# Seeding a PSUM bank with the epsilon term of an RMS norm, and one warm-up product less

## The chip, the cores and the metric

One core of one Trainium2 chip runs the whole program. The metric is the device time of one execution in microseconds (us); lower is better. A profiled execution gives a trace with one record for each instruction.

## The reference

```python
kv  = einsum('bhsd,bhse->bhde', k, v)            # q, k, v: 8 x 8 x 576 x 64, fp32
out = einsum('bhsd,bhde->bhse', q, kv)
rms = sqrt(mean(out * out, axis=-1) + 1e-06)     # over the 64 elements of a head
x   = (out / rms * g_norm)                       # reshaped to 4608 tokens x 512
h   = x @ w_in                                   # 512 x 2048
y   = 0.5 * h * (1 + erf(h / sqrt(2))) @ w_out   # gelu, then 2048 x 512
```

It is a linear attention without softmax, an RMS norm over each head, and a feed-forward layer.

## The kernel before

The 4608 tokens are cut into nine chunks of 512. For a chunk, `Attn` makes the transposed attention output in four head pairs `p` (128 partitions are two heads of 64, 512 columns are tokens), norms it, and splits the normed values into a high and a low part, on which the feed-forward layer runs: `layer1` (or `layer1_pair`) into `ps_h` banks, `gelu`, and `layer2` into four `acc` banks. The weights come as raw 64-bit words and are converted on the chip during the first chunk (`top_w` on ScalarE, `bits_w` on VectorE, `high_w` on ScalarE, `low_w` on VectorE). While one chunk runs through the feed-forward layer, the attention of the next is done between the products. The instructions of each engine run in the order in which the program issues them; nothing reorders them.

The first chunk has nothing to hide behind, and its attention is written out by hand before the loop. This is the stretch that the change touches:

1. `keep_warm(10)` issues ten products of a tile of zeros into a bank that nobody reads (`dummy`). A product of fp32 operands is two passes of TensorE, each with its own weight load, so these are 20 passes. Meanwhile GpSimd fills small constants (`mask`, `heads`, `ident`, `fold`), and the loads of k, v and q are on their way.
2. For each head pair `p`, `sum_first(p)` sums k times v over the batch's rows (line 145) and masks the result into `kv_f` on VectorE (line 622); `project_first(p)` multiplies it with q (line 630) and squares the result on ScalarE (line 634). A one-column product (line 649) turns `g_norm` into a per-partition scalar, `half_g` (line 650).
3. The sums of the squares of pairs 0 and 1 come from VectorE's `reduce` and a product with `fold` (line 665), those of pairs 2 and 3 from products with `heads` in `sum_squares` (line 641). All of them lie in one PSUM bank, `sums`: 48 columns, each written by a product that starts and ends its own sum.
4. `rsqrt` (lines 240 to 268) takes the inverse roots on VectorE: `m` = sums / 64 + epsilon (line 247), a first guess from the bits of `m` (line 250), and two polynomial refinements (`stt` at line 256, products with `m` at lines 261 and 265). That is nine instructions, each of which needs the one before.
5. TensorE meanwhile issues `keep_warm(2)`, the sums of k times v of the second batch (line 145 again), and `keep_warm(2)` once more. Then line 687 spreads the roots of pairs 2 and 3 over the tokens with 16 products with `ident`, 32 passes. VectorE spreads those of pairs 0 and 1 (line 277) and applies all of them (lines 695 and 705), and `layer1` starts on the normed values (line 512 for the first two of its blocks, in plain fp32).

Of the kernel before, what the change touches and what calls it, by code (L numbers as in the profile page):

```python
# [8 lines left out]
F32 = mybir.dt.float32  # L9
F32R = mybir.dt.float32r  # L10
I32 = mybir.dt.int32
AF = mybir.ActivationFunctionType
ALU = mybir.AluOpType
# [3 lines left out]
P = 128  # L17
EPS = 1e-6
# [17 lines left out]
def linear_attn_rms_gelu_ffn(  # L36
# [16 lines left out]
    nc = tc.nc  # L53
# [6 lines left out]
    D = g_norm.shape[0]  # L60
    NF = w_in.shape[0]
# [4 lines left out]
    const = ctx.enter_context(tc.tile_pool(name="const", bufs=1))  # L66
# [12 lines left out]
    half_g = const.tile([P, 1], F32, name="half_g")  # L79
    heads = const.tile([P, 2], F32, name="heads")  # L80
# [4 lines left out]
    def late_tile(name):  # L85

        if name not in late:
            late[name] = const.tile([P, 2 * DM], I32, name=name).bitcast(F32)
        return late[name]
# [45 lines left out]
    def sum_kv(b, pairs, ps=None):  # L135

        first = 0 if ps is not None else pairs[0]
        if ps is None:
            ps = kv_ps[b, first] = ps_a.tile([P, 512], F32, name="ps_a")
        for p in pairs:  # L140
            n = p - first
            for j, (k, v) in enumerate(kv_in.pop((b, p))):

                for r in (slice(0, D), slice(D, 2 * D)):
                    nc.tensor.matmul(  # L145
                        out=ps[r, n * D:(n + 1) * D], lhsT=k[:, r], rhs=v[:, r],
                        start=(j == 0), stop=(j == NJ),
                    )
# [12 lines left out]
    class Attn:  # L161
# [76 lines left out]
            )  # L238
            return ps

        def rsqrt(self, ps):

            m, y, t = (
                work.tile([P, NP * NB], F32, name=a, bufs=2)[:, :ps.shape[1]]
                for a in ("m", "y", "t")
            )
            nc.vector.tensor_scalar(
                out=m, in0=ps, scalar1=1.0 / D, scalar2=EPS, op0=ALU.mult, op1=ALU.add
            )
            nc.vector.tensor_scalar(  # L250
                out=y.bitcast(I32), in0=m.bitcast(I32), scalar1=-0.5, scalar2=RSQRT_MAGIC,
                op0=ALU.mult, op1=ALU.add,
            )

            def stt(out, in0, c, op0, in1):
                nc.vector.scalar_tensor_tensor(
                    out=out, in0=in0, scalar=c, in1=in1, op0=op0, op1=ALU.mult
                )

            stt(t, y, RSQRT_S2, ALU.mult, y)  # L260
            nc.vector.tensor_tensor(out=t, in0=t, in1=m, op=ALU.mult)
            stt(t, t, RSQRT_D1, ALU.add, t)
            stt(y, t, RSQRT_D0, ALU.add, y)
            stt(t, y, -0.125, ALU.mult, y)
            nc.vector.tensor_tensor(out=t, in0=t, in1=m, op=ALU.mult)
            stt(y, t, 1.5, ALU.add, y)
            return y
# [201 lines left out]
    def top_w(n):  # L469


        zs[n] = work.tile([P, DM], I32, name="z", bufs=2)
        top = raw[n].rearrange("p (n two) -> p n two", two=2)[:, :, 1]
        if n < FULL:
            z = late_tile(f"w_out{NF - 1}")[:, n * DM:(n + 1) * DM]
        else:
            z = work.tile([P, DM], F32, name="w", bufs=2)
        nc.scalar.activation(
            out=zs[n].bitcast(F32), in_=top.bitcast(F32), func=AF.Prelu,
            scale=2.0 ** -112, alpha=2.0 ** 32,  # L480
        )
        ws[n] = z.bitcast(I32)
# [79 lines left out]
    first, second = attn[:2]  # L562
    nc.vector.memset(warm, 0.0)
    nc.scalar.activation(out=heads, in_=warm[:, :2], func=AF.Gelu)
    mask, g_row = late_tile(f"w_in{NF - 6}")[:, :P], late_tile(f"w_in{NF - 6}")[:1, P:2 * P]
    nc.gpsimd.memset(mask, 0.0)
    for r in (slice(0, D), slice(D, 2 * D)):
        nc.gpsimd.memset(mask[r, r], 1.0)
    load_kv(0, 0)
# [26 lines left out]
    def keep_warm(count):  # L596
        for _ in range(count):
            nc.tensor.matmul(out=dummy[:, :P], lhsT=warm, rhs=warm, start=True, stop=True)  # L598

    sums = ps_h.tile([P, CH], F32, name="ps_h")  # L600
# [2 lines left out]
    nc.gpsimd.memset(heads, 0.0)  # L603
    for h in range(2):
        nc.gpsimd.memset(heads[h * D:(h + 1) * D, h:h + 1], 1.0)
    make_identity(nc, ident)
    for d in range(0, 2 * D, BLK):
        h = d // D * D
        nc.gpsimd.tensor_tensor(
            out=fold[:, d:d + BLK], in0=ident[:, h:h + BLK], in1=ident[:, h + BLK:h + 2 * BLK],  # L610
# [7 lines left out]
    sq, NG = {}, CH // P  # L618

    def sum_first(p):  # L620
        sum_kv(0, (p,))
        nc.vector.tensor_tensor(
            out=kv_f[:, p].rearrange("p (a n) -> p a n", a=2),
            in0=kv_ps.pop((0, p))[:, :D].unsqueeze(1).broadcast_to((P, 2, D)),
            in1=mask.rearrange("p (a n) -> p a n", a=2), op=ALU.mult,
        )

    def project_first(p):
        first.ps[p] = ps_acc.tile([P, DM], F32, name=f"acc{p}")
        nc.tensor.matmul(  # L630
            out=first.ps[p], lhsT=kv_f[:, p], rhs=first.q.pop(p), start=True, stop=True
        )
        sq[p] = work.tile([P, CH], F32, name=SQ[p], bufs=2 if p == 3 else None)
        nc.scalar.activation(out=sq[p], in_=first.ps[p], func=AF.Square)

    n = 2 * NB


    def sum_squares(p):
        for k in range((p - 2) * NG, (p - 1) * NG):  # L640
            nc.tensor.matmul(  # L641
                out=sums[:, n + 2 * k:n + 2 * k + 2],
                lhsT=sq[p][:, k % NG * P:(k % NG + 1) * P], rhs=heads, start=True, stop=True,
            )

    first.part = work.tile([P, NP, NB], F32, name="part")
    sum_first(0)
    ps = ps_a.tile([P, 512], F32, name="ps_a")
    nc.tensor.matmul(out=ps[:, :1], lhsT=g_row, rhs=heads[:1, :1], start=True, stop=True)
    nc.vector.tensor_scalar(  # L650
        out=half_g, in0=ps[:, :1], scalar1=0.5, scalar2=None, op0=ALU.mult
    )
    project_first(0)
    sum_first(1)
# [5 lines left out]
    for p in (2, 3):  # L660
        project_first(p)
    top_w(0)
    bits_w(0)
    sum_squares(2)
    nc.tensor.matmul(  # L665
        out=sums[:, :n].rearrange("p (g b) -> p g b", g=2), lhsT=fold, rhs=first.part[:, :2, :],
        start=True, stop=True,
    )
    sum_squares(3)
    for p in (2, 3):  # L670
        nc.scalar.activation(
            out=first.o_tile(p), in_=first.ps.pop(p), func=AF.Copy, scale=half_g
        )
    top_w(1)
    first.inv = first.rsqrt(sums[:, :n + 4 * NG])

    keep_warm(2)
    kv_ps[1, 0] = ps_a.tile([P, 512], F32, name="ps_a")
    sum_kv(1, (0, 1), kv_ps[1, 0])
    keep_warm(2)  # L680
    bcs = {}
    for p in (2, 3):
        bcs[p] = ps_acc.tile([P, DM], F32, name=f"acc{p}")
        for t in range(NG):
            for h, r in enumerate((slice(0, D), slice(D, 2 * D))):
                k = n + 2 * ((p - 2) * NG + t) + h
                nc.tensor.matmul(  # L687
                    out=bcs[p][r, t * P:(t + 1) * P],
                    lhsT=first.inv[:, k:k + 1].broadcast_to((P, D)), rhs=ident,
                    start=True, stop=True,  # L690
                )
    for p in range(2):
        bc = work.tile([P, CH], F32, name=SQ[p])
        first.spread(p, bc)
        nc.vector.scalar_tensor_tensor(
            out=first.o_tile(p), in0=first.ps.pop(p), scalar=half_g, in1=bc, op0=ALU.mult,
            op1=ALU.mult,
        )
        first.high_x(p)
        if p == 0:  # L700
            first.low_x(0, nc.gpsimd)
            top_w(2)
# [10 lines left out]
    g, h, acc, sums = {}, {}, {}, {}  # L713
# [121 lines left out]
    for s in range(PLAIN * NF):  # L835
# [36 lines left out]
        else:  # L872
# [3 lines left out]
            n = 0 if not 1 <= i <= 11 else 2 if i in (1, 3, 5, 7, 11) else 1  # L876
# [116 lines left out]
```

## Time and profile before

| | us |
|---|---|
| three runs | 836.53, 839.05, 838.25 |
| median of the three | 838.25 |
| the profiled execution | 836.58 |
| its span, first instruction to last | 834.80 |
| outside of the span | 1.78 |

The three runs lie 2.5 us apart, which is 0.3%. The span is what the trace shows; the time outside it is before the first and after the last instruction. TensorE passes are pipelined, so the length that the trace gives for one pass is longer than the distance between the starts of two, and the distance is what a pass costs in a row of them.

### The profile page before, as it was taken

To read this page: it belongs to the slowest core of one execution; us is meant where nothing else is said; L and a number is where in the kernel's file an instruction comes from. 1 tells how busy PE (TensorE), PEld (TensorE's weight loads), DVE (VectorE), ACT (ScalarE), POOL (GpSimd) and SP (SyncE) were. 2 spreads that over 40 slices of the span, in tenths; PEclk is the share of its full clock that TensorE was granted. 3 is DMA by queue.
4 is the path that set the end of the run, shared out by engine and by line. 5 is a ranking of instruction groups with operands and counts; after the bars stand their busy time and mean duration, and the time that the engine had idled before them with its cause. 6 is when DMAs were issued, how large, how long until landed. Compare 5 with 4: busy or idle time off the path is not lost.

```text
span 834.8 us, 13786 instructions
## 1 busy us (share of the span) xinstructions
PE 829.1 (99%) x5380; PEld 734.7 (88%) x5380; DVE 495.3 (59%) x980; ACT 314.2 (38%) x580; POOL 65.2 (8%) x67
## 2 busy tenths in 40 slices
PE   8999999999999999999999999999999999999998
PEld 7688888888999999999999999999999989999997
DVE  3999838687546744674457545673467446744442
ACT  2788444434531334233423253233323332322221
POOL 1000021011010101010001010010101000100000
PEclk9999999999999999999999999999999999999999
DMA  9981337776684568456955587456455655556551
GB/s 350 406 328 51 114 123 258 255 247 239 242 313 131 175 237 302 165 177 202 325 172 174 203 275 263 148 181 231 172 170 174 214 202 177 177 177 227 177 177 50
DMA packets 61460, 174.96 MB, mean 210 GB/s; under 512 B 6484, under 2 KB 15188, under 8 KB 61396
## 3 DMA queue, kind: packets, MB, share of 16 engines
q1 hardware_dynamic: 61392, 174.09, 59.8%
q8 instruction: 42, 0.69, 0.3%
q14 instruction: 22, 0.18, 0.1%
q10 hardware_dynamic: 4, 0.00, 0.0%
HBM read 149.95 MB, written 24.12 MB: 209 GB/s over the span
## 4 chain that ended last, share of the span: by engine, by line
PE 98%; DMA 1%; ACT 0%; issue 0%
PE acc L546 47%; PE ps_h L427 34%; PE ps_h L520 10%; PE ps_a L205 3%; PE ps_a L145 2%; DMA w_out<-kv_main 1%; PE ps_h L512 1%; PE acc L687 0%; PE acc L630 0%; PE ps_h L641 0%; PE ps_a L235 0%; PE ps_h L598 0%; ACT z L557 0%; PE ps_h L665 0%
## 5 line engine op out<-in xcount | busy, mean ns | idle before, releaser
L546 PE MATMUL acc<-w_out,gh 128*128 128x512 f32 x704 | 218.4, 392 | 0.0
L427 PE MATMUL ps_h<-w_in,w_in 128*128 128x256 f32 x1392 | 176.2, 283 | 0.0
L427 PEld LDWEIGHTS ps_h<-w_in,w_in 128*128 128x128 f32 x1392 | 171.1, 192 | 0.0
L546 PE MATMUL acc<-w_out,w_in 128*128 128x512 f32 x672 | 159.7, 392 | 0.0
L546 PEld LDWEIGHTS acc<-w_out,gh 128*128 128x128 f32 x704 | 130.1, 188 | 25.5
L546 PEld LDWEIGHTS acc<-w_out,w_in 128*128 128x128 f32 x672 | 124.1, 188 | 24.7
L546 PE MATMUL acc<-w_out,gl 128*128 128x512 f32 x352 | 137.2, 390 | 0.0
L532 ACT ACTIVATE gh<-ps_h 128x512 fp32r<-128x512 f32 x88 | 52.5, 597 | 212.6 <-DVE ps_h L419 155.3
L427 PEld LDWEIGHTS ps_h<-x,w_in 128*128 128x128 f32 x960 | 122.6, 191 | 4.4
L427 PE MATMUL ps_h<-x,w_in 128*128 128x256 f32 x960 | 123.9, 283 | 0.0
L532 ACT ACTIVATE w_in<-ps_h 128x512 fp32r<-128x512 f32 x56 | 33.5, 598 | 184.8 <-DVE ps_h L419 184.8
L437 DVE COPY w_in<-ps_h 128x256 f32<-128x256 f32 x56 | 23.8, 425 | 133.2 <-PE ps_h L427 133.2
L419 DVE TENSOR_TENSOR ps_h<-ps_h,w_in 128x256 f32<-128x256 f32 x168 | 72.7, 433 | 48.0 <-PE ps_h L427 43.6
L419 DVE TENSOR_TENSOR w_in<-ps_h,w_in 128x256 f32<-128x256 f32 x168 | 71.4, 425 | 49.1 <-PE ps_h L427 47.2
L520 PE MATMUL ps_h<-x,w_in 128*128 128x512 f32 x360 | 86.8, 390 | 0.0
L538 DVE TENSOR_TENSOR gl<-ps_h,gh 128x512 fp32r<-128x512 f32 x88 | 60.5, 687 | 42.7 <-ACT ps_h L533 38.2
L533 ACT ACTIVATE ps_h<-ps_h 128x512 f32<-128x512 f32 x144 | 85.4, 593 | 0.0
L520 PEld LDWEIGHTS ps_h<-x,w_in 128*128 128x128 f32 x360 | 67.5, 188 | 13.9 <-POOL x L290 0.2
L546 PEld LDWEIGHTS acc<-w_out,gl 128*128 128x128 f32 x352 | 66.1, 188 | 14.1
L538 DVE TENSOR_TENSOR w_in<-ps_h,w_in 128x512 fp32r<-128x512 f32 x56 | 38.5, 687 | 17.0 <-ACT ps_h L533 17.0
L193 POOL TENSOR_TENSOR ql<-q,qh 128x512 fp32r<-128x512 f32 x16 | 21.3, 1328 | 211.0 <-ACT qh L192 116.0
L325 POOL TENSOR_TENSOR w_in<-o,w_in 128x512 fp32r<-128x512 f32 x13 | 16.8, 1311 | 212.3 <-ACT w_in L320 212.3
(135 smaller groups left out, 635.5 us busy)
## 6 DMA issues: line engine op xcount, KB each, us to landing
w_in<-products SPq DMA_DIRECT2D x196, 512.0 KB, 4.7
products<-w_in SPq DMA_DIRECT2D x40, 256.0 KB, 3.2
kv_main<-kv_main SPq DMA_DIRECT2D x18, 512.0 KB, 6.7
w_in<-w_in SPq DMA_DIRECT2D x16, 512.0 KB, 10.2
w_out<-w_out SPq DMA_DIRECT2D x16, 512.0 KB, 10.2
q<-qT SPq DMA_DIRECT2D x15, 512.0 KB, 6.3
out<-w SPq DMA_DIRECT2D x18, 256.0 KB, 2.1
out<-z SPq DMA_DIRECT2D x18, 256.0 KB, 2.2
```

Of the source, the lines that this page charges most:

```text
L145: nc.tensor.matmul(out=ps[r, n * D:(n + 1) * D], lhsT=k[:, r], rhs=v[:, r], start=(j == 0), stop=(j == NJ),)
L193: eng.tensor_tensor(out=ql, in0=q, in1=qh.bitcast(F32), op=ALU.subtract)
L205: nc.tensor.matmul(out=ps[:, a:e], lhsT=w, rhs=x[:, a:e], start=(m == 0), stop=(m == 2))
L325: eng.tensor_tensor(out=x[:, 1], in0=self.block(OPERANDS[n]), in1=x[:, 0].bitcast(F32), op=ALU.subtract,)
L419: add = lambda out, x, y: nc.vector.tensor_tensor(out=out, in0=x, in1=y, op=ALU.add)
L427: nc.tensor.matmul(out=out, lhsT=y, rhs=x[:, z, kb], start=first and kb + i == 0, stop=kb == 1 and i == 2, skip_group_check=True,)
L437: nc.vector.tensor_copy(out=p1, in_=a[:, left])
L520: nc.tensor.matmul(out=h, lhsT=parts["in", i][:, w][:, p * P:(p + 1) * P], rhs=at.x[p][:, x], start=(m + p == 0), stop=(m == 2 and p == NP ...
L532: nc.scalar.activation(out=gh, in_=h, func=AF.Gelu)
L533: nc.scalar.activation(out=h, in_=h, func=AF.Gelu)
L538: nc.vector.tensor_tensor(out=gl, in0=h, in1=gh.bitcast(F32), op=ALU.subtract)
L546: nc.tensor.matmul(out=ps, lhsT=x[:, ts], rhs=parts["out", i][:, w], start=(i == 0 and m == 0), stop=(i == NF - 1 and m == 2),)
```

## The change

A row of ones and a row of 64 times epsilon are filled by GpSimd. One product of the two, with one row of contraction, writes 64 times epsilon into all 48 columns of `sums` before the first sum; the sums of squares then accumulate on it. `rsqrt` takes its roots from that bank as it stands, which gives roots smaller by the factor 8 (the square root of 64), and a scalar `root_g` = 8 times `half_g` takes the place of `half_g` where the first chunk is scaled. The second `keep_warm(2)` becomes `keep_warm(1)`.

```diff
-        def rsqrt(self, ps):
+        def rsqrt(self, ps, ready=False):
...
-            nc.vector.tensor_scalar(
-                out=m, in0=ps, scalar1=1.0 / D, scalar2=EPS, op0=ALU.mult, op1=ALU.add
-            )
+            if ready:
+                m = ps
+            else:
+                nc.vector.tensor_scalar(
+                    out=m, in0=ps, scalar1=1.0 / D, scalar2=EPS, op0=ALU.mult, op1=ALU.add
+                )
...
+    ones, eps = (late_tile(f"w_in{NF - 6}")[:1, a * P:(a + 1) * P] for a in (2, 3))
...
+    nc.gpsimd.memset(ones, 1.0)
+    nc.gpsimd.memset(eps, D * EPS)
     make_identity(nc, ident)
...
-                lhsT=sq[p][:, k % NG * P:(k % NG + 1) * P], rhs=heads, start=True, stop=True,
+                lhsT=sq[p][:, k % NG * P:(k % NG + 1) * P], rhs=heads, start=False, stop=True,
+                skip_group_check=True,
...
+    nc.tensor.matmul(
+        out=sums[:, :n + 4 * NG], lhsT=ones, rhs=eps[:, :n + 4 * NG], start=True, stop=False,
+        skip_group_check=True,
+    )
     sum_first(0)
...
+    root_g = const.tile([P, 1], F32, name="root_g")
+    nc.vector.tensor_scalar(
+        out=root_g, in0=half_g, scalar1=D ** 0.5, scalar2=None, op0=ALU.mult
+    )
     project_first(0)
...
         out=sums[:, :n].rearrange("p (g b) -> p g b", g=2), lhsT=fold, rhs=first.part[:, :2, :],
-        start=True, stop=True,
+        start=False, stop=True, skip_group_check=True,
...
-            out=first.o_tile(p), in_=first.ps.pop(p), func=AF.Copy, scale=half_g
+            out=first.o_tile(p), in_=first.ps.pop(p), func=AF.Copy, scale=root_g
...
-    first.inv = first.rsqrt(sums[:, :n + 4 * NG])
+    first.inv = first.rsqrt(sums[:, :n + 4 * NG], True)
...
     sum_kv(1, (0, 1), kv_ps[1, 0])
-    keep_warm(2)
+    keep_warm(1)
...
-            out=first.o_tile(p), in0=first.ps.pop(p), scalar=half_g, in1=bc, op0=ALU.mult,
+            out=first.o_tile(p), in0=first.ps.pop(p), scalar=root_g, in1=bc, op0=ALU.mult,
```

## Rows read from the trace of the kernel before

**Rows 1.** The page of the profile: busy time and share of the span by engine, and the shares of the chain of work that ended last by engine.
```profile
PE 829.1 (99%) x5380; PEld 734.7 (88%) x5380; DVE 495.3 (59%) x980; ACT 314.2 (38%) x580; POOL 65.2 (8%) x67
PE 98%; DMA 1%; ACT 0%; issue 0%
```

**Rows 2.** All waits of TensorE between 12 us and the end of the span: who waited for whom, us in total, times, longest.
```profile
PE ps_a L145 <- DMA w_out<-kv_main: 0.2, 1, 0.2
```

**Rows 3.** The chain of work that ended last, in order of time, from 4 to 28 us: start, length, what.
```profile
4.34 7.31 DMA w_out<-kv_main
11.64 0.14 issue
11.78 0.80 PE ps_a L145 x20
...
18.42 0.64 PE ps_h L598 x4
19.06 1.96 PE acc L687 x32
21.02 7.15 PE ps_h L512 x16
```

**Rows 4.** VectorE in order of time, 15.7 to 20.4 us: start, length, line, operation, tiles; in brackets the idle time before and what ended it (none where there is no bracket).
```profile
16.18 0.69 DVE L491 SCALAR_TENSOR_TENSOR w_out<-w_in,w_out 128x512 int32<-128x512 int32 x1
16.78 0.20 DVE L247 TENSOR_SCALAR m<-ps_h 128x48 f32<-128x48 f32 x1
17.02 0.19 DVE L250 TENSOR_SCALAR y<-m 128x48 int32<-128x48 int32 x1
...
18.46 0.21 DVE L265 TENSOR_TENSOR t<-t,m 128x48 f32<-128x48 f32 x1
18.70 0.21 DVE L256 SCALAR_TENSOR_TENSOR y<-t,y 128x48 f32<-128x48 f32 x1
18.94 0.71 DVE L277 STREAM_TRANSPOSE sq<-y 128x512 f32<-128x512 f32 x1
```

**Rows 5.** TensorE's passes (PE) and weight loads (PEld) in order of time, 15.2 to 21 us, neighbours of one kind merged (xcount).
```profile
15.27 0.30 PEld L665 LDWEIGHTS ps_h<-part,fold 128*128 128x128 f32 x2
15.52 1.03 PE L641 MATMUL ps_h<-heads,gh 128*128 128x2 f32 x8
16.39 0.53 PEld L598 LDWEIGHTS ps_h<-warm 128*128 128x128 f32 x4
18.35 0.52 PEld L598 LDWEIGHTS ps_h<-warm 128*128 128x128 f32 x4
18.35 0.71 PE L598 MATMUL ps_h<-warm 128*128 128x128 f32 x4
19.02 1.75 PEld L687 LDWEIGHTS acc<-ident,y 128*64 128x64 f32 x32 [0.15 <-issue]
20.95 0.30 PEld L512 LDWEIGHTS ps_h<-o,w_out 128*128 128x128 f32 x2 [0.17 <-issue]
```

**Rows 6.** Two lines of `rsqrt` over the whole span: ns shortest/median/longest, first and last start, shapes and their counts. The bank `ps_a` or `ps_h` is PSUM, `m` is SBUF.
```profile
L247 DVE TENSOR_SCALAR m<-ps_a x8: 215/215/225, 91.2 to 697.2; 128x64 f32<-128x64 f32 x8
L247 DVE TENSOR_SCALAR m<-ps_h x1: 201/201/201, 16.8 to 16.8; 128x48 f32<-128x48 f32 x1
L250 DVE TENSOR_SCALAR y<-m x9: 188/195/196, 17.0 to 697.5; 128x64 int32<-128x64 int32 x8, 128x48 int32<-128x48 int32 x1
```

**Rows 7.** TensorE's passes in order of time, 0 to 12.5 us, before the chain of rows 3 is TensorE's.
```profile
1.06 4.64 PE L598 MATMUL ps_h<-warm 128*128 128x128 f32 x20 [1.06 <-DVE warm L563]
5.62 0.88 PE L145 MATMUL ps_a<-w_out 112*64 112x64 f32 x16
6.55 0.38 PE L649 MATMUL ps_a<-heads,w_in 1*128 1x1 f32 x2
7.09 1.13 PE L630 MATMUL acc<-w_in,w_in 128*128 128x512 f32 x2 [0.16 <-DVE w_in L622]
8.55 0.69 PE L145 MATMUL ps_a<-w_out 112*64 112x64 f32 x16 [0.34 <-DMA w_out<-kv_main]
9.74 1.12 PE L630 MATMUL acc<-w_in,w_in 128*128 128x512 f32 x2 [0.38 <-DVE w_in L622]
11.78 0.69 PE L145 MATMUL ps_a<-w_out 112*64 112x64 f32 x16 [0.18 <-DMA w_out<-kv_main]
```

**Rows 8.** GpSimd and the ScalarE queue's load of `g_norm`, in order of time, 0.7 to 5.7 us.
```profile
0.74 0.20 POOL L566 MEMSET w_in<- 128x128 f32 x1 [0.29 <-POOLq L983]
1.00 0.33 POOL L568 MEMSET w_in<- 64x64 f32 x2
1.05 0.74 ACTq L578 DMA_DIRECT2D w_in<-g_norm  x2
2.36 0.10 POOL L603 MEMSET heads<- 128x2 f32 x1 [1.03 <-ACT heads L564]
2.53 0.24 POOL L605 MEMSET heads<- 64x1 f32 x2
5.32 0.31 POOL L615 MEMSET kv_l<- 64x256 f32 x1
```

**Rows 9.** VectorE's other instructions around the change and after it, in order of time.
```profile
6.96 0.16 DVE L650 TENSOR_SCALAR half_g<-ps_a 128x1 f32<-128x1 f32 x1
9.39 0.29 DVE L622 TENSOR_TENSOR w_in<-ps_a,w_in 128x128 f32<-128x128 f32 x1 [2.27 <-PE ps_a L145]
30.44 0.68 DVE L503 TENSOR_TENSOR w_in<-w,w_in 128x512 fp32r<-128x512 f32 x1
```

**Rows 10.** Weight loads of the first layer's plain blocks and of its first split block (line 520), in order of time; and one wait of ScalarE for a transfer of weights in the stretch between.
```profile
21.90 0.30 PEld L512 LDWEIGHTS ps_h<-o,w_out 128*128 128x128 f32 x2 [0.65 <-DVE o L695]
22.49 0.19 PEld L512 LDWEIGHTS ps_h<-o,w_out 128*128 128x128 f32 x1 [0.29 <-DVE o L705]
32.05 2.68 PEld L520 LDWEIGHTS ps_h<-x,w_in 128*128 128x128 f32 x12
30.07 0.70 ACT L478 ACTIVATE z<-w_in 128x512 f32<-128x512 f32 x1 [1.11 <-DMA w_in<-w_in]
```

[...]

## The prediction made before the run

> **What bounds the kernel now.** I read the page first: TensorE is busy in 99% of the span, and 98% of the chain that ended last is its work [rows 1]. The reader is to see that no other engine's average matters; a saving counts only if TensorE's own sequence gets shorter, or if TensorE stands still somewhere for what is saved. The second view, TensorE's waits, leaves one wait of 0.2 us after 12 us [rows 2]. The third, the chain in order of time, shows where that one lies: until 11.64 us the chain is the load of the last k and v of the first batch, and from 11.78 us on it is TensorE, pass after pass, to the end [rows 3]. So the change has two halves with different prices. What it adds lies at 2 to 8 us, before the load ends, and is free as long as it stays inside TensorE's waits for the loads. What it removes lies at 16.8 to 19 us, on TensorE's chain.
>
> The fourth view shows who really sets the pace there. On the chain stand four passes of zeros (line 598, the second `keep_warm(2)`) and then the 32 passes of line 687 [rows 3]. The zeros need nothing and nobody reads them; line 687 needs the roots. VectorE's chain of `rsqrt` has its last instruction from 18.70 to 18.91 us, and line 687's first weight load starts at 19.02 us, 0.11 later [rows 4, 5]. The loads of the four zero passes run from 18.35 to 18.87 us, and then the weight path idles for 0.15 us [rows 5]. So at 19.02 us TensorE is waiting for VectorE, and the zero passes only fill what the wait leaves. The pace-setter of this spot is `rsqrt`, nine instructions in a row.
>
> **What the change removes.** The first of the nine, line 247, goes. It starts at 16.78 us and the next starts at 17.02: one link of the chain is 0.24 us [rows 4]. What could keep line 250 from starting at 16.78 instead? It would need the sums, whose last pass ends at 16.55 (15.52 + 1.03, rows 5), and VectorE, which is on the first weight block's bits (line 491) from 16.18 to 16.87 with no idle time reported before line 247 [rows 4]. So VectorE is the later of the two, and line 250 can take line 247's place. Gross: -0.24 us.
>
> Against it: lines 250, 261 and 265 now read PSUM where they read `m` from SBUF. No row shows these three with a PSUM operand. The nearest is line 247 against line 250, the same kind of instruction on the same shape: 201 ns from PSUM against 188 from SBUF, and 215 against 195 with 64 columns in place of 48 [rows 6]. That is 13 to 20 ns each, 0.04 to 0.06 for three; the lower end is nothing, if the 13 ns belong to the operation and not to the bank. I take 0.04. Net: -0.20 us, between -0.18 and -0.24.
>
> [...]
>
> **The two dummy passes.** Four weight loads of zeros take 0.52 us here and 0.53 at 16.39 [rows 5], the last of them about 0.19 as in [rows 10], so they start 0.11 apart. With the roots ready at 18.71 and the same 0.11 after them, line 687 could start at 18.82. With all four zero passes it would start after 18.87, so only 0.15 of the 0.20 would be had. With two, their loads end near 18.65 and line 687 goes at 18.82. The removal is worth 0.05 and leaves an idle time of 0.17 before line 687, about the 0.15 of now.
>
> **Does the gain reach the end?** Line 512 starts behind line 687's passes; its second and third operands wait for VectorE's lines 695 and 705 [rows 10]. VectorE's spread starts at 18.94, 0.03 after the last root, and the two that follow stand on it, so these waits end 0.20 earlier too. Next is the conversion of the weights, which is paced by transfers: ScalarE waits 1.11 us for one at 30.07 [rows 10], and that does not move. But it is not late: the low half of the third block's weights is done at 31.12 (30.44 + 0.68, rows 9), and TensorE wants it in the fifth of 12 passes that begin at 32.05 [rows 10], nearly 2 us later. With 0.20 us less there is still room, and the waits view shows none after it. So the gain goes through to the end.
>
> **What the change adds.** Each with its cover:
> - The seed product: two passes and weight loads before `sum_first(0)`. The nearest rows are the dummy passes before it, 20 in 4.64 us, 0.23 each [rows 7], and those at 18.35, 0.11 each; 0.2 to 0.46 together. I take the upper end: it stands right behind the slow ones. The sums at 5.62 would start up to 0.46 late. The next sums, at 8.55, now wait 0.34 for their load, so 0.12 is left; the sums at 11.78 wait 0.18 for theirs [rows 7]. The whole is gone there. Cost to the end: 0. Without these two waits it would be 0.46.
> - Two fills on GpSimd behind line 605. One partition of 128 columns; the nearest rows are 0.10 (128x2) and 0.20 (128x128) [rows 8]. They end by 3.2 us at the latest (2.77 + 0.40), and the seed product is not due before 5.6. GpSimd's queue behind them ends at 5.63 and shifts by 0.2 to 0.4; its results, `fold` and `ident`, are first read at 15.27 and 19.02 us [rows 5]. Cost 0.
> - `root_g` on VectorE, like `half_g` 0.16 us, behind 6.96 + 0.16; VectorE's next work is at 9.39 after 2.27 us of idling [rows 9]. Cost 0.
> - Accumulating in place of starting sums, in the same 18 passes: nothing is issued or waited for anew.
> - The bank `sums` is read until line 265's new place, 18.4 us, in place of 17.0; its next writer is line 512 at 20.95 [rows 5]. Cost 0.
>
> **The sum.** 836.58 - 0.24 + 0.04 = 836.38 us for an execution like the profiled one, a span of 834.60. That execution is 1.67 below the median of the runs shown; the same step from the median gives 838.25 - 0.20 = 838.05 us. The three runs lie 0.3% apart, and about 0.3%, 2.5 us, is what a measurement of this kernel can tell from no change. The gain is a tenth of that.
>
> **The rivals.**
> 1. *PSUM reads cost more than the rows suggest*, as much as line 247 did, so `rsqrt` is as long as before and only the wait before line 687 grows. For it: lines 261 and 265 with one operand in either memory are shown by no row. Against: the 13 to 20 ns of rows 6. Time: 838.25, no change. [...]
> 2. *The seed product comes late.* `ones` and `eps` lie in the tile that also takes `g_norm` by DMA. If their fills waited for that transfer, which no row shows landing before its reader at 6.55, the sums would start at 6.55 + 0.46 in place of 5.62: 1.39 late, less 0.34 and 0.18 of waits, 0.87 late on the chain, net +0.67, 838.92 us. It decides from 0.72 us of lateness on (0.34 + 0.18 + the 0.20 of gain). Against it: the DMA for `g_norm` was issued at 1.05 while fills of the same tile ran from 1.00 to 1.33 [rows 8], so work on other parts of one tile does not wait.
> 3. *TensorE's pace falls* because fewer zeros are multiplied: slower, the other side. [...] It decides once the idle time before line 687 is longer than those that TensorE has already gone through at the quick pace: 0.34 before 8.55 and 0.38 before 9.74, after which two passes of line 630 took 1.12, as at 7.09 [rows 7]. I work out 0.17, so it should not.
> 4. *The gain is swallowed later*, by a transfer that paces the weights: 838.25. Against it are the 2 us of room above.
>
> **How the numbers follow.** The forecast 0.78, rival 1 0.08, rival 2 0.05, rival 3 0.03, rival 4 0.06. Only rival 3 is out of the 0.3% by itself. The scatter of the runs can carry a median by most of 0.3% either way, more easily down with a gain in hand: I give 0.05 to faster, 0.04 to slower (0.03 of it rival 3), 0.91 to the same. The range is the lowest and the highest run moved by the gain, 836.3 and 838.9, the upper end raised to 839.2 for rival 2.
>
> **What would show it.** In the changed trace line 250 starts at about 16.8 with no line 247 before it; lines 250, 261 and 265 take within 0.02 us of their present 0.19 and 0.21; line 687's first load starts at about 18.8, and line 512's at about 20.75; the sums at 11.78 start as before; the span is some 834.6. The prediction is wrong if the sums at 11.78 start later, if lines 261 and 265 take 0.27, if line 512's passes stand further apart, or if TensorE shows a new wait after 30 us.

## The result and the profile after

The changed kernel is slower: 841.58 us median of seven runs (841.07 to 845.62) against 837.56 for the kernel before (836.50 to 839.05), a ratio of 1.0061 with a 95% interval of [1.0045, 1.0077]. The forecast was 838.05, with 0.91 on no change. The profiled execution took 844.69 us, a span of 842.9 where the one before had 834.8. Two single executions, one of 1369 us (of the kernel with 512 unused bytes) and one of 4197 us (of the kernel before, beside the variants), count in none of the ratios and counts below.

The page of the changed kernel: busy time by engine, and the chain that ended last by engine.

```profile
PE 837.4 (99%) x5380; PEld 734.5 (87%) x5380; DVE 495.9 (59%) x980; ACT 314.8 (37%) x580; POOL 65.0 (8%) x69
PE 97%; DMA 2%; SPq 0%; ACT 0%; issue 0%
```

TensorE issues as many passes as before, 5380 [rows 1], and is busy 8.3 us longer. So all but a little of the extra time (0.3 us for a load, below) is not a wait. It is passes that take longer, and it comes in two pieces. They part where line 512 (now 515) begins and where it ends. In both traces the lines of TensorE, VectorE, ScalarE and GpSimd follow one another in the order of the program over the whole span (in the trace before, 244, 576, 508 and 29 stretches of one line).

The first piece, up to 31 us. Instructions of the changed kernel in order of time: start, length, engine, line, operation; in brackets the idle time before.

```profile
5.63 0.66 PE L655 MATMUL ps_h<-w_in 1*128 1x48 f32 x2
6.22 1.03 PE L145 MATMUL ps_a<-w_out 112*64 112x64 f32 x16
11.78 0.64 PE L145 MATMUL ps_a<-w_out 112*64 112x64 f32 x16
16.73 0.20 DVE L253 TENSOR_SCALAR y<-ps_h 128x48 int32<-128x48 int32 x1
18.32 1.12 PE L145 MATMUL ps_a<-kv_main 112*64 112x64 f32 x16 [0.31 <-DMA kv_main<-kv_main]
18.66 0.71 DVE L280 STREAM_TRANSPOSE sq<-y 128x512 f32<-128x512 f32 x1
20.31 3.68 PE L703 MATMUL acc<-ident,y 128*64 128x128 f32 x32
```

The seed product is covered as forecast: the sums at 11.78 start at 11.78 [rows 7]. The roots are done 0.28 earlier than before (18.66 against 18.94 of rows 4). But line 703 (line 687 before) starts at 20.31 in place of 19.06, and its 32 passes take 3.68 us in place of 1.96 [rows 3]. The granted clock says why. Four stretches of the changed kernel: start and end, length; busy time and instructions of PE, PEld, VectorE, ScalarE, GpSimd; TensorE's granted clock (1.00 is the full one); DMA share; GB/s:

```profile
16.00:17.00 1.00, 1.00 (x10) 0.88 (x12) 0.93 (x4) 0.78 (x2) 0.00 (x0) 1.00 1.02 368
17.00:18.00 1.00, 1.00 (x20) 0.82 (x20) 0.86 (x5) 0.00 (x0) 0.00 (x0) 0.63 1.04 416
22.00:24.00 2.00, 2.00 (x21) 1.67 (x17) 0.69 (x1) 1.08 (x2) 0.53 (x1) 0.50 1.05 397
24.00:26.00 2.00, 2.00 (x5) 1.04 (x6) 1.86 (x4) 1.17 (x2) 0.00 (x0) 0.98 1.02 406
```

From 17.3 us to 24.1 us TensorE runs at a granted clock of 0.50, the lower of the two levels that the traces show. It fell before line 602's two dummy passes, which come at 19.58. By the start of line 515 the execution is 3.0 us behind that of before (23.92 against 20.95 of rows 5), though its load of the second batch also came 0.31 late.

The second piece, after 31 us. The chain of work that ended last, 53 to 62 us, in both kernels: start, length of a group of 12 passes, line (549 is line 546 before, 523 is 520). Before:

```profile
53.38 2.72 PE acc L546 x12
56.10 2.72 PE ps_h L520 x12
```

After:

```profile
54.10 2.80 PE ps_h L523 x12
56.90 2.79 PE acc L549 x12
```

Each group of twelve 512-column passes takes 0.08 us longer, at a granted clock of 1.00. The first two chunks hold 61 such groups (30 of line 523, 31 of line 549). After them come the paired chunks, whose first layer has passes of 256 columns (line 427 before, 430 now), 42 in a row. Before:

```profile
209.76 5.03 PE ps_h L427 x42
236.18 5.46 PE acc L546 x24
```

After:

```profile
217.12 5.00 PE ps_h L430 x42
243.52 5.60 PE acc L549 x24
```

From the first pass of line 512 to the first of line 427, 21.02 to 209.76 us in the chain before and 23.99 to 217.12 in the chain now, 4.4 us are lost. Behind it only 0.7 are, because two effects nearly cancel there: the second layer's passes that read `gh` and `gl` are slower (24 of them 5.60 in place of 5.46), and the first layer's groups of 42 are faster (4.95 to 5.00 over the whole span, in place of 5.03). With the 3.0 of the first piece this is the span's 8.1 us. Executions at full clock show the second piece alone: 841.07 to 841.58, some 4.6 us above the 836.8 that the kernel before took at full clock in a later measurement.

### The profile page after: what moved, and what is told of

It is laid out like the page before. It is cut to its first block, busy times and chain, and to the rows that moved or that the text cites. A ratio compares the mean times of both kernels' runs of the same rounds, so it can differ in the third digit from the quotient of the medians.

```text
span 842.9 us, 13788 instructions
## 1 busy us (share of the span) xinstructions
PE 837.4 (99%) x5380; PEld 734.5 (87%) x5380; DVE 495.9 (59%) x980; ACT 314.8 (37%) x580; POOL 65.0 (8%) x69
## 4 chain that ended last, share of the span: by engine, by line
PE 97%; DMA 2%; SPq 0%; ACT 0%; issue 0%
PE acc L549 48%; PE ps_h L430 33%; PE ps_h L523 10%; PE ps_a L205 3%; PE ps_a L145 2%; DMA kv_main<-kv_main 1%; PE ps_h L515 1%; DMA w_in<-qT 1%; PE acc L703 0%; PE ps_a L235 0%; SPq L115 0%; PE ps_h L602 0%; ACT z L560 0%; SPq L173 0%; SPq L120 0%
## 5 line engine op out<-in xcount | busy, mean ns | idle before, releaser
L549 PE MATMUL acc<-w_out,gh 128*128 128x512 f32 x704 | 222.2, 397 | 0.0
L549 PE MATMUL acc<-w_out,gl 128*128 128x512 f32 x352 | 139.1, 395 | 0.0
L430 PEld LDWEIGHTS ps_h<-x,w_in 128*128 128x128 f32 x960 | 120.1, 188 | 4.7
L430 PE MATMUL ps_h<-x,w_in 128*128 128x256 f32 x960 | 121.3, 279 | 0.0
L523 PE MATMUL ps_h<-x,w_in 128*128 128x512 f32 x360 | 89.0, 395 | 0.0
L523 PEld LDWEIGHTS ps_h<-x,w_in 128*128 128x128 f32 x360 | 67.4, 188 | 16.0
```

The source lines that it names most:

```text
L430: nc.tensor.matmul(out=out, lhsT=y, rhs=x[:, z, kb], start=first and kb + i == 0, stop=kb == 1 and i == 2, skip_group_check=True,)
L523: nc.tensor.matmul(out=h, lhsT=parts["in", i][:, w][:, p * P:(p + 1) * P], rhs=at.x[p][:, x], start=(m + p == 0), stop=(m == 2 and p == NP ...
L549: nc.tensor.matmul(out=ps, lhsT=x[:, ts], rhs=parts["out", i][:, w], start=(i == 0 and m == 0), stop=(i == NF - 1 and m == 2),)
```

## What the runs compare

Neither of the two pieces was among the steps worked out, so they were tested apart. In the compiled program each tile has its byte address in its partition. Before, the tiles `x0` to `x5` lie behind the last weight tile, and the working tiles (`gh` and `gl` among them) behind those. Between the weight tiles and these lie whole multiples of 256 bytes, as the sizes of the tiles give them in the order in which the kernel allocates them: `w_in0` to `x0` 98,304 (24 weight tiles of 4,096), `w_out0` to `gh` 135,424. The tile `root_g` has 4 bytes, takes a 32-byte slot ahead of `x0`, and moves all of `x` and the working tiles up by 32. Theory 1 was that this move makes the passes longer; the rival, that the seeded bank, the accumulation or the missing dummy product does. For the clock, theory 3 was the missing dummy product, and the rival that it falls by chance whatever is changed there.

### Only the addresses, without the change

```diff
         out=half_g, in0=ps[:, :1], scalar1=0.5, scalar2=None, op0=ALU.mult
     )
+    pad = const.tile([P, 1], F32, name="pad")
+    nc.gpsimd.memset(pad, 0.0)
```

> The kernel before with nothing changed but an unused tile of one column (a 32-byte slot) where the change puts root_g. Theory 1, addresses: the groups of twelve passes in the first two chunks go from 2.72 to 2.80 us and the time rises by 4.5 to 5 us to 841.5 to 843. Theory 2: nothing but addresses changes, so the groups stay at 2.72 and the time stays at 837 to 838.

841.83 us median, ratio 1.0048 [1.0030, 1.0065]. The chain of this kernel:

```profile
51.32 2.80 PE ps_h L520 x12
54.12 2.79 PE acc L546 x12
```

An unused tile of 4 bytes reproduces the loss, in time and in the groups, without anything that the change computes. The rival has fallen for the second piece.

### root_g in 64 bytes

```diff
-    root_g = const.tile([P, 1], F32, name="root_g")
+    root_g = const.tile([P, 16], F32, name="root_g")[:, :1]
```

> The changed kernel with one edit: root_g gets 16 columns (64 bytes) in place of one, so every tile behind it in SBUF starts at a multiple of 64 bytes again, as before the change, where one column takes a 32-byte slot. Theory 1, addresses: the groups of twelve 512-column passes of the first two feed-forward chunks go back from 2.80 to 2.72 us, 62 groups give back 4.8 us, and the undisturbed time is 836.4 to 837.5, the level of the kernel before. Theory 2, the pace is slow because of what the change computes (the seeded bank, the accumulation, one dummy product less): the groups stay at 2.80 and the time stays at 841 to 842. Either way single executions may lose another 1 to 4 us where the clock falls near 17 us.

844.20 us median, ratio 1.0070 [1.0052, 1.0088], where theory 1 gave 836.4 to 837.5. In the profile the groups of line 523 took 2.76 and 2.79 and those of line 549 2.79 to 2.80.

```profile
50.61 2.76 PE ps_h L523 x12
53.37 2.79 PE acc L549 x12
```

So theory 1 was right about the cause and wrong about its form: it isn't the remainder of an address modulo 64. Four of the six executions had a mean clock (the granted clock averaged over the span) of 0.998 or less, and the median lies higher for it; the profiled one, at 1.000, took 841.77.

### All tiles moved together

```diff
     heads = const.tile([P, 2], F32, name="heads")
+    pad = const.tile([P, 16], F32, name="pad")
+    nc.gpsimd.memset(pad, 0.0)
```

> The kernel before with an unused tile of 64 bytes ahead of all weights, x tiles and working tiles: all of them move from 64 past a multiple of 128 to a multiple of 128 bytes. Theory 1a, only the remainder modulo 64 matters: 837 to 838, groups of twelve passes at 2.72 us. Theory 1b, the remainder modulo 128 matters too: the groups change from 2.72, in either direction, by the 0.08 that 32 bytes cost or more; if faster, towards 2.6, the kernel would gain some 10 us or more.

838.05 us, ratio 0.9998 [0.9987, 1.0009], groups at 2.72 with a few at 2.75 and 2.76.

```profile
54.61 2.72 PE acc L548 x12
57.33 2.72 PE ps_h L522 x12
```

With this kernel `x0` lies 64 bytes further on, just where the run with 64 bytes for `root_g` had it. The one is fast and the other slow; what differs is where the weights lie. So it is a distance that counts.

### The distance, from 64 to 512 bytes

The same unused tile as in the first run, with 16, 32, 64 and 128 columns.

> The kernel before with an unused 64-byte tile where the change puts root_g: the same distances as in the changed kernel with root_g in 64 bytes. Distances: the groups of line 520 at 2.76 and 2.79 and those of line 546 at 2.80 as there, undisturbed executions at 841 to 842. If only the remainder of each address modulo 64 counted, 2.72 and 837.

> The kernel before with an unused 128-byte tile where the change puts root_g. 256 and 512 bytes left the groups of twelve passes at 2.72 us, 32 and 64 made them 2.76 to 2.80. If the distance between weight and x or working tiles counts modulo 128: 2.72. If it counts modulo 256: between 2.74 and 2.80.

> The kernel before with an unused 256-byte tile there. If distances count modulo 256 (or a divisor of it): 2.72 and 837. If any shift against the weights costs: 2.76 to 2.80 and 841 or more.

> The kernel before with an unused 512-byte tile there. Modulo 512 or a divisor: 2.72 and 837. If 256 is slow and this one fast, the distance counts modulo 512; if both are slow, modulo 1024 or more.

64 bytes: 842.68 us, 1.0060 [1.0040, 1.0079]. 128 bytes: 844.51 in one execution with a mean clock of 0.998, so here the groups tell more than the time. 256 bytes: 837.59, 1.0010 [0.9997, 1.0024]. 512 bytes: 837.19, 0.9994 [0.9980, 1.0008]. The chains with 64, 128, 256 and 512 bytes, two rows each, in this order:

```profile
54.25 2.79 PE acc L546 x12
57.04 2.79 PE ps_h L520 x12
```
```profile
55.32 2.80 PE acc L546 x12
58.12 2.80 PE ps_h L520 x12
```
```profile
56.74 2.72 PE acc L546 x12
59.46 2.72 PE ps_h L520 x12
```
```profile
52.85 2.72 PE acc L546 x12
55.57 2.72 PE ps_h L520 x12
```

32, 64 and 128 bytes cost; 256 and 512 are free. As far as these five values show, the distance counts modulo 256.

### The change with nothing moved

```diff
-    half_g = const.tile([P, 1], F32, name="half_g")
+    g2 = const.tile([P, 2], F32, name="half_g")
+    half_g, root_g = (g2[:, a:a + 1] for a in range(2))
...
-    root_g = const.tile([P, 1], F32, name="root_g")
```

> The changed kernel with root_g as the second column of half_g's 32-byte slot, so that no tile moves: every address is that of the kernel before. Theory 1 in its new form, distances: what counts is how far the x and working tiles lie from the weight tiles, which before the change were whole multiples of 256 bytes; groups of twelve passes in the first two chunks return to 2.72 us and an undisturbed execution takes 836.3 to 837.3. Theory 2, the change's own work makes them slow: 2.79 to 2.80 and 841 or more. Against the kernel before, the 0.24 us of the removed link should be seen in the trace and not in the times.

836.80 us against 837.19 of the kernel before, measured beside it, ratio 0.9996 [0.9980, 1.0013]. Executions with a mean clock above 0.998 have their median at 836.36 here and at 836.82 in the kernel before. Its rows: the roots on VectorE, line 687's counterpart (line 703), the first layer's first load, and two groups of the chain.

```profile
16.78 0.20 DVE L254 TENSOR_SCALAR y<-ps_h 128x48 int32<-128x48 int32 x1
17.25 0.20 DVE L265 TENSOR_TENSOR t<-t,ps_h 128x48 f32<-128x48 f32 x1
18.22 0.20 DVE L269 TENSOR_TENSOR t<-t,ps_h 128x48 f32<-128x48 f32 x1
18.70 0.71 DVE L281 STREAM_TRANSPOSE sq<-y 128x512 f32<-128x512 f32 x1
```
```profile
18.79 1.75 PEld L703 LDWEIGHTS acc<-ident,y 128*64 128x64 f32 x32 [0.20 <-issue]
20.71 0.30 PEld L516 LDWEIGHTS ps_h<-o,w_out 128*128 128x128 f32 x2 [0.17 <-issue]
```
```profile
53.14 2.72 PE acc L550 x12
55.86 2.72 PE ps_h L524 x12
```

With the slot alone taken away, what the prediction worked out for the trace stands there: line 254 at 16.78, line 703 at 18.79 (18.82 was worked out), line 516 at 20.71 in place of 20.95, the groups at 2.72. The change itself gains 0.24 us on TensorE's chain, and nothing that a time can show. That the roots begin at 16.78 in both traces is luck: in the other traces without a fall of the clock they begin between 16.25 and 17.26. The distance from there to the first layer's first load is steadier: 4.16 to 4.17 in four traces with the old roots (4.31 and 4.51 in two more), and 3.93 to 3.94 in three with the new ones (5.02 in the one whose load came late, below).

### Which tiles: x alone, all working tiles, gh alone

The kernel before, with 64 unused bytes ahead of the tiles named and, but for the working tiles, 192 behind them, so that the rest moves by 256. The edit for x alone:

```diff
+    pad = const.tile([P, 16], F32, name="pad")
+    nc.gpsimd.memset(pad, 0.0)
+    for a in range(6):
+        const.tile([P, 2, CH], F32R, name=f"x{a}")
+    back = const.tile([P, 48], F32, name="back")
+    nc.gpsimd.memset(back, 0.0)
```

> The kernel before with 64 unused bytes ahead of the six x tiles and 192 behind them: the x tiles lie 64 bytes off, gh and gl lie 256 bytes off, which was free. If it is the distance between the two operands of a pass: line 520, which reads x and a weight tile, has its groups at 2.76 to 2.79, and line 546, which reads gh or gl and a weight tile, stays at 2.72; 30 groups by 0.055 us are 1.6 us more. If it is some other traffic in SBUF that the shift disturbs: both lines change, or neither.

> The kernel before with 64 unused bytes behind the x tiles: x stays where it was, all working tiles (gh and gl among them) lie 64 bytes off. If the two operands of a pass must lie a multiple of 256 bytes apart: line 546 goes to about 2.80 a group, line 520, which reads x and weights alone, stays at 2.72. If the pass is disturbed by other engines' traffic in the working tiles: both slow.

> The kernel before with 64 unused bytes ahead of gh and 192 behind it: gh alone lies 64 bytes off, x in place, all else 256 bytes off, which was free. If it is the two operands of a pass: of each group of line 546 the eight passes that load gh slow by about 6 ns each and the four that load gl don't, so the group takes about 2.77, and line 520 stays at 2.72. If it is the writing of gh by ScalarE or its reading by VectorE beside the passes: line 520 slows as well.

x alone: 841.34 us in one execution, whose mean clock was 0.996, so the time says little; line 520 at 2.76 to 2.81 and line 546, which doesn't read x, at 2.75 to 2.77. All working tiles: 843.80, 1.0084 [1.0069, 1.0100]; line 546 at 2.79 to 2.80, line 520, which reads none of them, at 2.73 to 2.77. gh alone: 843.33, 1.0064 [1.0048, 1.0081]; line 546 at 2.79 to 2.80 where 2.77 was expected, line 520 at 2.73 to 2.75. Chains of the three, in this order:

```profile
54.58 2.80 PE ps_h L520 x12
57.38 2.76 PE acc L546 x12
```
```profile
54.25 2.80 PE acc L546 x12
57.05 2.75 PE ps_h L520 x12
```
```profile
53.46 2.79 PE acc L546 x12
56.26 2.75 PE ps_h L520 x12
```

Both plain readings fail in part. The passes that read a moved tile beside an unmoved weight are slowed, and moving gh alone costs line 546 as much as moving all working tiles. But the line that reads no moved tile is slowed too, by less: 0.01 to 0.05 a group. Where in the group this happens can be read from the starts of the passes. The first four and the last four passes of the group at 56.10 in the run with gh alone:

```profile
56.10 1.09 PE L520 MATMUL ps_h<-x,w_in 128*128 128x512 f32 x4
57.94 1.07 PE L520 MATMUL ps_h<-x,w_in 128*128 128x512 f32 x4
```

Behind a group of line 546 the first five passes of line 520 start 231, 236, 228, 232 and 231 ns apart, and all others 227 or 226, the pace of the kernel before (medians of 24 groups). The kernel before has such a run-in too, behind passes of another kind: its groups of line 546 behind line 145 show 231, 236, 228, 232 and 230 from their second pass on, then 227. In the run with x alone the groups of line 546 behind line 145 settle at 227 as soon as that, and behind line 520 only after ten passes. So what the untouched line loses lies in a run-in behind the slowed group. That speaks against the other engines' work on the moved tiles, which would not end with it. What makes a run-in stays open.

In the paired chunks the groups are longer and the effects stand apart. With x alone moved, the second layer's groups of 24 take 5.47 as before, and the first layer's 42 take 4.99 and 5.02 in place of 5.03: there the move makes passes faster. With all working tiles moved, the groups of 24 that read `gh` and `gl` take about 5.60 and those that read tiles among the weights, which didn't move, stay at 5.47; the 42 hardly change (5.02 to 5.04). From the first pass of line 427 to the end it is 625.0 us before, 623.7 with x alone moved, 628.7 with all working tiles moved and 625.8 with both (32 bytes). So moving the working tiles alone costs more (843.80) than moving x with them (841.83).

### The dummy passes and the clock

```diff
     sum_kv(1, (0, 1), kv_ps[1, 0])
-    keep_warm(1)
+    keep_warm(2)
```

This edit was made twice: in the version with 64 bytes for `root_g`, and in the one with `root_g` in `half_g`'s slot.

> The changed kernel with root_g in 64 bytes and the second keep_warm back at two products (four passes). Theory 3, the missing two dummy passes let the clock fall near 17 us: no execution of this kernel shows a mean granted clock under 1.000, while some of the kernel with 64 bytes and two passes do. Theory 4, the clock falls for a reason that lies ahead of the dummy passes (it fell at about 17.4 us, they start at 18.35) or by chance: executions with a clock under 1.000 turn up here too, or in the kernel before. In an undisturbed execution the time is 0.05 above that of the version with two passes, which cannot be told from none.

> The changed kernel with root_g in half_g's slot and the second keep_warm back at two products. As worked out before the run: line 687's counterpart starts where the four weight loads of zeros end, at about 18.87 on the profile's scale of the kernel before, 0.05 to 0.10 later than with two. Rival: the removed product is what brought the whole gain, and the start stays at 19.02.

With 64 bytes: 842.17 us, 1.0052 [1.0033, 1.0072]. Two of six executions had a mean clock of 0.998 or less, with all four passes in place. The kernel with all tiles moved together, which has the four passes too, fell in its profile: the stretch from 17 to 18 us.

```profile
17.00:18.00 1.00, 1.00 (x22) 1.00 (x22) 0.85 (x5) 0.00 (x0) 0.00 (x0) 0.50 0.98 397
```

All six kept traces with a mean clock of 0.998 or less have one fall, which begins between 16.9 and 18.2 us; five of the six kernels have all four dummy passes. Of the kernel before no trace with a fall was kept, but 30 of its 76 executions beside the variants had a mean clock of 0.998 or less. Theory 3 has fallen: the removed product isn't what lowers the clock. A fall costs 1 to 4 us in most executions: in 29 of the kernel before measured together, the median was 836.82 above 0.998, and they took 837.8 to 839.1 at 0.998 and 840.3 to 842.3, up to 5.5 us more, at 0.995 to 0.996.

The second run, one execution of 837.60, doesn't measure what it was meant to. The load of the second batch came late in it:

```profile
18.23 0.55 PEld L146 LDWEIGHTS ps_a<-kv_main 112*64 112x64 f32 x16 [0.89 <-DMA kv_main<-kv_main]
18.41 0.71 DVE L281 STREAM_TRANSPOSE sq<-y 128x512 f32<-128x512 f32 x1
18.96 0.52 PEld L603 LDWEIGHTS ps_h<-warm 128*128 128x128 f32 x4
19.60 0.63 PEld L703 LDWEIGHTS acc<-ident,y 128*64 128x64 f32 x12
```

The roots are ready at 18.37 and line 703 starts 0.12 behind the four zero loads, which end at 19.48. Here it is TensorE that holds the start, and the two passes more cost an estimated 0.22 (two loads 0.11 apart) rather than 0.05. What they cost where the load is in time wasn't seen.

### Columns in the passes ahead of the fall

Made on the version with `root_g` in `half_g`'s slot. The wider `heads` moves the weight, x and working tiles all together, by 512 bytes.

```diff
-    heads = const.tile([P, 2], F32, name="heads")
+    heads = const.tile([P, P + 8], F32, name="heads")[:, :P]
...
-                out=sums[:, n + 2 * k:n + 2 * k + 2],
+                out=sums[:, n + 2 * k:n + 2 * k + P],
```

> The changed kernel with root_g in half_g's slot, and the products of the sums of squares (line 641's counterpart) with 128 columns in place of 2: 126 columns of zeros behind the two of heads, which are added as zeros to columns already seeded or not read. A pass there is set by its weight load (0.11 us), and the dummy passes of 128 columns start 0.11 apart too, so the passes should cost nothing. Theory: the clock falls near 17 us in some executions because TensorE, though occupied, multiplies almost nothing from 14.4 to 16.4 us; with columns in these passes no execution falls there, all lie at 836.0 to 837.2 and the mean is about 1 us under that of the kernel before. Rival: the fall depends on something else; 839.5 to 841 with a mean clock of 0.995 to 0.996 turn up in one execution of four as in the version without.

836.57 us against 837.62 of the kernel before, measured beside it, ratio 0.9987 [0.9976, 0.9997]: the one version whose interval lies below 1. None of its 12 executions had a mean clock under 0.999. Beside it 8 of 17 of the kernel before had 0.998 or less, and of the same version with two columns 3 of 12, in another measurement. The passes cost nothing that shows, as expected: eight weight loads of line 648 take 0.97 us, as before the change (line 641, shown first).

```profile
14.38 0.97 PEld L641 LDWEIGHTS ps_h<-heads,ql 128*128 128x128 f32 x8 [0.72 <-issue]
```
```profile
14.43 0.97 PEld L648 LDWEIGHTS ps_h<-heads,ql 128*128 128x128 f32 x8 [0.66 <-ACT ql L641]
```

The result fits the theory that the falls have to do with the two columns a pass from 14.4 to 16.4 us. It isn't shown: it is twelve executions of one version, 0 of 12 against 3 of 12 can be chance, and no run took the columns away elsewhere to make a fall.

## Why the prediction was wrong

**The step that failed** is the term for `root_g`: "on VectorE, like `half_g` 0.16 us, behind 6.96 + 0.16; VectorE's next work is at 9.39 ... Cost 0." The instruction costs nothing indeed: it took 0.15 us in the idle time. Its tile was not costed: the term was put at nothing by looking at the engine alone. It is the only new tile with a slot of its own (`ones` and `eps` lie in an old one), it moved some twenty others by 32 bytes against the weight tiles, and that is the whole 4.6 us: the same tile without the change costs it (841.83), and the change without the tile doesn't (836.80). No row of the trace before could have priced this, but the diff shows a new allocation ahead of tiles that TensorE reads, and no end of the range was kept for it.

**The link of `rsqrt`**: right, and a little better than worked out. In the run with nothing moved the reads of PSUM took 200, 203 and 204 ns where the same lines took 188, 209 and 209 from SBUF before, on the same shape. The one-operand form lost 12 ns and the two-operand forms gained 5 to 6, so the net is 0.24 us and not 0.20. Rival 1 falls with these reads. The 0.27 us that the prediction names for lines 261 and 265 is shown by no run: they took 0.203 and 0.204.

**The two dummy passes**: the start at 18.79 in the run with nothing moved fits the 18.82 worked out, but what their removal is worth by itself (0.05) wasn't measured.

**The cover of the seed product**: right, and tested harder than forecast. In the changed kernel's profile the sums that follow it started at 6.22 in place of 5.62, 0.60 late against the 0.46 allowed, and those at 11.78 still started at 11.78. Its fills did not wait for `g_norm`: GpSimd ran them at 2.80 and 2.94 us. Rival 2 falls.

**The pace of TensorE**, rival 3, was right that a slower pace could come, and wrong on place, cause and price. It falls near 17 us, before the dummy passes that were taken away, and by the mean clocks in the kernel before too. It costs mostly 1 to 4 us. That rival 3 alone lies out of the 0.3% rested on an estimate, about 7 us for line 512's 16 passes (7.15 us, rows 3) at half their pace, which no run shows. The prediction looked for the fall in idle times; 0.38 us of idling had left the pace as it was. The zero passes at the start ran at the lower pace: they start 0.213 us apart, each 0.421 long in the trace, and the last three of the four at 18.35 start 0.111 and 0.112 apart. The view of that stretch, in the columns given above, has a granted clock of 1.00:

```profile
0.00:5.60 5.60, 4.54 (x20) 4.34 (x20) 0.17 (x1) 1.49 (x2) 3.50 (x20) 1.00 0.65 226
```

But no record of the clock stands in that trace ahead of 6.08 us, so this 1.00 is no reading. The sums at 5.62 show the change of pace: a pair of their passes starts every 0.107 us from 5.79 to 6.00, and every 0.058 from 6.10 on. In the changed kernel's trace, whose first record lies at 7.03 us, it is 0.107 from 6.38 to 7.02, and 0.060 from 7.09 on. The prediction took the scatter of the three runs, 2.5 us, for noise; their clocks aren't on record, but later executions of this kernel with a mean above 0.998 lie within 1.2 to 2.3 us of each other, where all of a measurement lie within 3.5 to 6.1.

**The gain reaching the end**: right, by the run with nothing moved (span 834.5 against 834.8, line 516 0.24 earlier; one execution of each). Rival 4 falls.

## What to carry to other kernels

A diff that allocates a tile can move the tiles behind it, here some twenty by 32 bytes: before costing such an edit, list where the tiles lie that TensorE reads, and put small new values into spare bytes of a slot that is already there. When a neutral edit costs a constant few per cent per pass over a long stretch, at full clock and without a wait, test the addresses with an unused tile before looking for a cause in the edit's work. The sign isn't the same everywhere: the move that slowed the 512-column passes made the first layer's 256-column passes 1% faster (42 in 4.95 to 5.00 us in place of 5.03). Where runs of one kernel scatter, sort them by their mean granted clock first. Passes with few columns whose weight loads set the pace took 126 columns more at no cost that shows here (eight loads in 0.97 us either way).

## What the runs showed of the hardware that was not expected

- Passes of 512 columns ran 2.72 us a dozen where the x and working tiles lay multiples of 256 bytes from the weight tiles, and 2.76 to 2.81 where they lay 32, 64 or 128 bytes off; moving all three kinds together by 64 bytes left them at 2.72, with a few at 2.75 and 2.76. Some 0.0067 us a pass, 3%, at most. A group that reads no moved tile lost 0.01 to 0.05, all of it in the first passes behind a slowed group.
- Passes of 256 columns that read x went the other way: 42 in a row took 5.03 us where x lay a multiple of 256 bytes from the weight tiles, and 4.95 to 5.00 where it lay 32 bytes off. Passes of line 512 (plain fp32, 0.43 apart) showed no difference: 7.20 us for 16 against 7.22.
- TensorE's granted clock fell from 1.00 to 0.50 between 16.9 and 18.2 us in all six kept traces with a mean clock of 0.998 or less; 30 of 76 executions of the kernel before had such a mean. It held through idle times of 0.34 and 0.38 us and fell after passes that followed each other from 14.4 to 16.4 us with two columns each. With 128 columns in those passes no mean was under 0.999 in 12.
- Three reads of PSUM by VectorE in place of SBUF, on 128x48, changed an instruction by +12, -6 and -5 ns.
